# Variance of one LayerNorm tile by a Square with a sum on ScalarE, in a new order of the first phase

## The chip, the cores and the metric

The kernel runs on one core of one Trainium2 chip. The metric is device time in microseconds (us) of one launch, the median over several runs. The core's engines each take their own queue of instructions in order: TensorE (PE, matmuls; its weight loads are shown as PEld), VectorE (DVE), ScalarE (ACT), GpSimd (POOL), and SyncE (SP), which here only issues transfers. They wait for each other through semaphores.

## What is computed

The reference normalises x, a 2048 x 512 matrix in bf16, and adds to x the outputs of two branches that both read the normalised rows:

```python
xn = layernorm(x)                          # over the 512 columns, eps = 1e-5
# branch A: linear attention, 32 heads of 16
q, k, v = split(xn @ wqkv)
pq, pk = phi(q), phi(k)                    # phi(t) = where(t > 0, t + 1, exp(t)) + 1e-6
num = pq @ (pk.T @ v)                      # per head
den = pq . sum(pk) + 1e-6
A = (num / den) @ wo
# branch B: SwiGLU, inner width 1792
B = (silu(xn @ w_gate) * (xn @ w_up)) @ w_down
out = x + A + B
```

## The kernel before

The 2048 rows are cut into 16 tiles of 128 rows, numbered 0 to 15, one row per partition. Phase 1 loads the tiles, normalises each, brings it into transposed form, projects it to k and q, applies phi, and accumulates the product of the normalised tile and phi(k) over all tiles. After that come the gate and up projections of the first 384 rows, the rest of the feed-forward branch in a form that saves products, and the output. The diff touches phase 1 alone, which in the trace lasts until about 48.7 us.

The order of the work in phase 1 is written out by hand: a string of steps, each a letter and a tile number, in the call of `run` at line 536. A step appends its instructions to the queue of the engine that it belongs to. So the place of a step in the string matters only against other steps on the same engine; between engines, the program `_Program.add` (line 53) derives from declared reads and writes which instruction waits for which, and each engine stops at the first instruction whose operands are not there.

The steps that matter below, with tile t:

- S(t), lines 307 and 310, DVE: the statistics of a tile of x (`bn_stats`) and their aggregate `mv`, mean and variance.
- M1, line 334, ACT: a Copy of tile 1 scaled by -1/512 with its sum, which is minus the mean (`negm`).
- R(t), lines 314 and 316, ACT: Ln of the variance plus eps, then Exp of -0.5 times that: `rstd`.
- r(t), lines 321 to 323, ACT: three small operations on one column, `std`, `r2` (one over the variance) and `lstd`. o(t), POOL, makes `flo` and `cap` from `std` (lines 326 and 329).
- Tiles 0 and 1 take a short way: they are only centred (a0, b0: halves of tile 0 on DVE, line 339; C1: tile 1 on DVE with `negm`, line 349), transposed and projected, and the scale `rstd` comes in later, in phi. N0 is a small POOL operation for tile 0.
- The other tiles are normalised in full: L(t) on DVE (line 377), P(t) on POOL (lines 392 and 395), A(t) on ACT.
- c0, d0 (halves of tile 0), W1, W3, X2: transposes on TensorE into a bank of PSUM (line 407). e0 on ACT (line 415), f0, w1, w3, Z2 on DVE (line 417): copies of these banks back to SBUF. From tile 5 on, D(t) on SP transposes by a transfer instead (line 423).
- K(t), k(t): first and second half (two matmuls each for tiles 0 to 3; from tile 4 on k(t) is all four) of the projection to k; Q(t), q(t) the same for q (line 444). Each projection takes the next of banks 4 to 7 in a ring: K0 has 4, K1 5, Q1 6, Q3 7, K3 4 again, then K2 5, Q0 6 and Q2 7.
- x(t), y(t) on ACT: Exp of a projection to k or q (lines 462 and 465). z(t) on ACT: a copy of the q projection (line 454). m(t), n(t) on POOL: a minimum (line 472). s(t) on DVE: phi(k), which reads the bank for the last time and so frees it (line 483); u(t) the same for q.
- J(t) on POOL for tiles 0 and 1: the mean negated into `nmg` (line 369), then xg = (x - mean) times `r2` (line 372), which G(t) needs. G(t), line 493, four matmuls: the product of phi(k) and the normalised tile, accumulated in banks 0 to 3.
- F2: two matmuls on constants that keep TensorE busy (line 297), after eight that stand ahead of the string.

Of the kernel before, what the change touches and what calls it, by code (L numbers as in the profile page):

```python
# [121 lines left out]
def bass_parallel_sum__linear_attn_block__swiglu_ffn__prompt_kernel(nc, A_x, A_wqkv, A_wo, B_x, B_w_gate, B_w_up, B_w_down, out):  # L122
    xin = A_x[0]
    oview = out[0]
    K = _Program()
    bf, f32 = dt.bfloat16, dt.float32

    with contextlib.ExitStack() as es:
        E = es.enter_context

        def sb(name, shape, dtype):
            return E(nc.sbuf_tensor(name, shape, dtype))

# [25 lines left out]
        M = sb("M", [P, NG, D], bf)  # L159
# [112 lines left out]
        for t in range(4, 16):  # L272
# [5 lines left out]
            out=ident[:, :], in_=ident[:, :], compare_op=ALU.not_equal, fill=1.0,  # L278
# [24 lines left out]
        def xk(t):  # L303
            return [("x", 0, 0), ("x", 0, 1)] if t == 0 else [("x", t)]
# [6 lines left out]

        def rs(t):
            sl = slice(t, t + 1)
            K.add("act", lambda e: e.activation(lnv[:, sl], mv[:, t, 1:2], ACT.Ln, bias=eps5[:, :], scale=1.0),
                  r=[("mv", t), ("eps5",)], w=[("lnv", t)])
            K.add("act", lambda e: e.activation(rstd[:, sl], lnv[:, sl], ACT.Exp, scale=-0.5),
                  r=[("lnv", t)], w=[("rs", t)])

# [14 lines left out]
        def neg_mean(t):  # L333
            K.add("act", lambda e: e.activation(
                junk, x_sb[:, t, :], ACT.Copy, scale=-1.0 / D, accum_out=negm[:, t:t + 1]),
                r=xk(t), w=[("negm", t), ("junk",)])

        def centre_half(t, h):
            K.add("dve", lambda e: e.tensor_scalar(
                out=xc[:, t, h * H:(h + 1) * H], in0=x_sb[:, t, h * H:(h + 1) * H], scalar1=mv[:, t, 0:1], scalar2=None,  # L340
                op0=ALU.subtract), r=xk(t) + [("mv", t)], w=[("xc", t, h)])
# [24 lines left out]
                op0=ALU.subtract, op1=ALU.mult), r=xk(t) + [("mv", t), ("r2", t)], w=[("xg", t)])  # L366

        def xg_pool(t):
            K.add("pool", lambda e: e.tensor_scalar(
                out=nmg[:, t:t + 1], in0=mv[:, t, 0:1], scalar1=-1.0, scalar2=0.0, op0=ALU.mult, op1=ALU.add),  # L370
                r=[("mv", t)], w=[("nmg", t)])
            K.add("pool", lambda e: e.tensor_scalar(
                out=xg[:, t, :], in0=x_sb[:, t, :], scalar1=nmg[:, t:t + 1], scalar2=r2[:, t:t + 1],
                op0=ALU.add, op1=ALU.mult), r=xk(t) + [("nmg", t), ("r2", t)], w=[("xg", t)])

        def lna_dve(t):
            K.add("dve", lambda e: e.tensor_scalar(
                out=xn[:, t, :], in0=x_sb[:, t, :], scalar1=mv[:, t, 0:1], scalar2=rstd[:, t:t + 1],
                op0=ALU.subtract, op1=ALU.mult), r=xk(t) + [("mv", t), ("rs", t)], w=[("xn", t)])
# [156 lines left out]
        run("""
            S0 M1 a0 b0 c0 R0 d0 F2 C1 S3 e0 N0 W1 r0 K0 o0 f0 R3 w1 S2 K1 P3 k0 S1 R2 J0 W3 x0 k1 Q1 L2 R1 w3
            m0 X2 q1 r1 Z2 Q3 s0 x1 o1 q3 S5 y1 K3 m1 k3 R5 n1 s1 G0 z1 L5 J1 x3 S9 K2 D5 Q0 z3 m3 S4 k2 R9 q0
            y3 P9 s3 G1 x2 S8 R4 m2 D9 Q2 z0 q2 P4 s2 R8 k5 z2 L8 n3 D4 S15 q5 x5 y0 S12 m5 G2 D8 y5 s5 q9 y2
            n5 S10 R15 k9 n0 y9 u5 R12 n9 k4 x9 L15 u9 D15 q4 m9 x4 L12 R10 s9 m4 q8 y4 D12 S11 P10 k8 z8 s4  # L540
            n4 R11 D10 G9 S13 x8 N11 A11 G5 m8 u4 y8 n2 s8 D11 G3 R13 S14 A0 P13 k15 S7 R14 k12 n8 D13 x15 L14
            S6 m15 q10 x12 D14 s15 m12 k10 y10 s12 n10 k11 x10 u10 R7 m10 q15 x11 s10 q11 m11 y15 L7 R6 s11
            D7 n15 k13 y11 u15 q13 n11 x13 L6 u11 D6 m13 q14 y13 s13 n13 q12 y14 u13 n14 k14 y12 u14 n12 q7
            x14 u12 m14 k7 y7 L1 s14 D0 D1 n7 k6 x7 u0 m7 q6 u7 x6 s7 m6 G4 y6 s6 n6 G12 u2 G14 u6 u1 G6 u8 G10
            u3 G11 G15 G8 G13 G7
        """)
        fload("sp", "wg", wg, B_w_gate, 1)
        wload("sp", 2)
# [304 lines left out]
        X1, X2 = slice(T0, T0 + TB), slice(T0 + TB, S)  # L853
# [507 lines left out]
```

## Time and profile before

| | us |
|---|---|
| median of 3 runs | 199.21 |
| lowest, highest run | 199.07, 199.49 |
| the profiled execution, its own time | 199.49 |
| its span, first to last instruction | 198.2 |
| TensorE busy | 193.8 |
| VectorE busy | 170.6 |
| ScalarE busy | 157.3 |
| GpSimd busy | 127.6 |

The profile is of one execution. The span is shorter than the time by what lies around the program, 1.3 us here. A row of a timeline gives the start and the duration of one instruction, or of a group of like instructions that follow each other, from the start of the first to the end of the last; the last entry is the idle time of the engine before it and what ended that. Instructions on one engine overlap a little at their ends, so a start can lie ahead of the end above it.

### The profile page before, as it was taken

Reading aid. Unit: us, or ns where it says so; the run is one execution under the profiler, and the core shown is the slowest. Engines: PE = TensorE matmul, PEld = TensorE weight load, DVE = VectorE, ACT = ScalarE, POOL = GpSimd, SP = SyncE. Lnnn points to the kernel's source line nnn. Section 1 sums busy time; section 2 is a strip of 40 time slices with the busy share of each in tenths; the row PEclk is TensorE's granted clock in tenths of the full one; section 3 lists DMA queues with packets and bytes.
Section 4 is the critical chain, followed back from the end, with each engine's and each line's share of the span. In section 5 each row is a group of like instructions: output and inputs, shape, how many; then the busy total and the mean of one; then the engine's idle time right before and its main releaser. Section 6 shows DMA issues by size and latency. Waiting matters only on the chain.

```text
span 198.2 us, 3561 instructions
## 1 busy us (share of the span) xinstructions
PE 193.8 (98%) x1193; PEld 115.2 (58%) x1207; DVE 170.6 (86%) x328; ACT 157.3 (79%) x314; POOL 127.6 (64%) x158
## 2 busy tenths in 40 slices
PE   8899999999999999999999999999999999999995
PEld 2344444444655555555555555555555888888884
DVE  2999998896997799887888998887888999998886
ACT  3799888699698998898999888998897967575300
POOL 3687877799999487689778877868579004413220
PEclk9999999999999999999999999999999999999999
DMA  5943248799900000111110221111000012132223
GB/s 171 360 131 81 61 86 231 211 275 373 348 14 0 3 0 0 28 26 30 28 26 2 55 53 26 26 26 31 2 0 2 3 40 66 33 77 66 45 65 121
DMA packets 28899, 15.97 MB, mean 81 GB/s; under 512 B 17232, under 2 KB 28880, under 8 KB 28880
## 3 DMA queue, kind: packets, MB, share of 16 engines
q1 hardware_dynamic: 28320, 15.28, 28.1%
q10 hardware_dynamic: 560, 0.46, 0.7%
q8 instruction: 9, 0.15, 0.3%
q14 instruction: 10, 0.08, 0.1%
HBM read 9.70 MB, written 2.10 MB: 60 GB/s over the span
## 4 chain that ended last, share of the span: by engine, by line
PE 94%; DVE 2%; DMA 2%; issue 1%; ACT 0%; POOL 0%; SPq 0%
PE pb L896 35%; PE pb L1104 16%; PE pb L444 13%; PE pb L565 9%; PE pb L493 7%; PE pb L719 6%; PE pb L1110 5%; DMA x_sb<-in_A_x_dram 2%; PE pb L723 2%; PE pb L625 0%; PE pb L711 0%; DVE pq L483 0%; PE pb L407 0%; POOL ef L472 0%; DVE stats L307 0%
## 5 line engine op out<-in xcount | busy, mean ns | idle before, releaser
L691 POOL TENSOR_TENSOR pq<-pq,rden 128x512 bf16<-128x512 bf16 x16 | 16.9, 1056 | 36.2 <-DVE rden L684 26.7
L896 PE MATMUL pb<-xnT,wgu 128*128 128x416 bf16 x112 | 26.6, 339 | 0.0
L444 PE MATMUL pb<-wqkv,xnT 128*128 128x512 bf16 x110 | 25.1, 379 | 0.2
L665 POOL TENSOR_TENSOR pz<-pq,zbc 128x512 f32<-128x512 bf16 x16 | 18.9, 1180 | 5.1 <-ACT pz L658 3.5
L565 PE MATMUL pb<-xnT,wgu 128*128 128x384 bf16 x112 | 19.9, 326 | 0.1
L931 DVE TENSOR_TENSOR pb<-p,pb 128x416 f32<-128x416 f32 x28 | 16.6, 595 | 3.6 <-PE pb L896 1.9
L472 POOL TENSOR_SCALAR ef<-ef 128x512 bf16<-128x512 bf16 x25 | 15.5, 620 | 5.8 <-ACT ef L465 5.6
L926 ACT ACTIVATE zacc<-pb,iw 128x416 bf16<-128x416 f32 x28 | 16.4, 614 | 3.1 <-PE pb L896 2.3
L444 PEld LDWEIGHTS pb<-wqkv,xnT 128*128 128x128 bf16 x112 | 10.9, 98 | 13.4 <-DVE pk L483 0.4
L936 DVE TENSOR_TENSOR c<-pb,p 128x416 f32<-128x416 f32 x28 | 16.4, 588 | 2.3 <-PE pb L896 0.3
L465 ACT ACTIVATE ef<-pb 128x512 bf16<-128x512 f32 x25 | 14.8, 593 | 3.9 <-PE pb L444 3.9
L940 POOL TENSOR_TENSOR hT<-c,zacc 128x416 bf16<-128x416 f32 x16 | 15.3, 974 | 2.3 <-ACT zacc L926 1.7
L510 POOL TENSOR_TENSOR zacc<-zacc,pk 128x512 f32<-128x512 f32 x13 | 16.0, 1232 | 1.0
L906 ACT ACTIVATE pb<-pb 128x416 f32<-128x416 f32 x28 | 13.7, 501 | 3.0 <-PE pb L896 1.9
L896 PEld LDWEIGHTS pb<-xnT,wgu 128*128 128x128 bf16 x112 | 10.9, 98 | 8.7
L921 ACT ACTIVATE zacc<-pb,iw 128x416 bf16<-128x416 f32 x28 | 15.7, 626 | 0.0
L565 PEld LDWEIGHTS pb<-xnT,wgu 128*128 128x128 bf16 x112 | 10.8, 98 | 7.0 <-DVE xn L613 0.2
L1104 PE MATMUL pb<-wgu,xnT 128*128 128x256 f16 (+1 forms) x112 | 14.9, 273 | 0.0
L896 PE MATMUL pb<-xnT,wqkv 128*128 128x416 bf16 x56 | 14.4, 339 | 0.3
L896 PE MATMUL pb<-wo,wqkv 128*128 128x416 f16 x56 | 14.4, 339 | 0.0
L896 PE MATMUL pb<-GT,wqkv 128*128 128x416 f16 x56 | 14.4, 339 | 0.0
L307 DVE BATCH_NORM_STATS2 stats<-x_sb 128x6 f32<-128x512 bf16 x16 | 10.8, 678 | 3.2 <-DMA x_sb<-in_A_x_dram 3.2
(202 smaller groups left out, 494.1 us busy)
## 6 DMA issues: line engine op xcount, KB each, us to landing
x_sb<-in_A_x_dram SPq DMA_DIRECT2D x14, 128.0 KB, 3.8
wgu<-in_B_w_gate_dram SPq DMA_DIRECT2D x2, 896.0 KB, 5.2
wgu<-in_B_w_up_dram SPq DMA_DIRECT2D x2, 896.0 KB, 8.0
wd<-in_B_w_down_dram SPq DMA_DIRECT2D x2, 896.0 KB, 13.1
out_dram<-out_sb SPq DMA_DIRECT2D x24, 64.0 KB, 1.6
wqkv<-in_A_wqkv_dram SPq DMA_DIRECT2D x3, 256.0 KB, 4.4
wqkv<-in_A_wqkv_dram SPq DMA_DIRECT2D x1, 512.0 KB, 6.3
wo<-in_A_wo_dram SPq DMA_DIRECT2D x1, 512.0 KB, 8.8
```

The lines of the kernel that those rows point to most:

```text
L444: K.add("pe", [(lambda e, c=c: e.matmul(banks[b][:, :], src[:, c, t * P:(t + 1) * P], wqkv[:, c, col:col + D], start=(c == 0), stop=(c == ...
L472: K.add("pool", lambda e: e.tensor_scalar(out=buf, in0=buf, scalar1=top, scalar2=0.0, op0=ALU.min, op1=ALU.max), r=[bkey] + tkeys, w=[bkey])
L510: K.add("pool", lambda e: e.tensor_tensor(out=dst, in0=acc, in1=more, op=ALU.add), r=[key, mkey], w=[dkey])
L565: fns.append(lambda e, c=c, b=b, w_=w_: e.matmul(banks[b][:, 0:T0], w_[:, c, fc * P:(fc + 1) * P], xnT[:, c, 0:T0], start=(c == 0), stop=( ...
L665: K.add("pool", lambda e: e.tensor_tensor(out=halves(i), in0=two(pq[:, t, :]), in1=two(zbc[:, :]), op=ALU.mult), r=[("pq", t), ("zbc",)] + ...
L691: K.add("pool", lambda e: e.tensor_tensor(out=heads(pq[:, t, :]), in0=heads(pq[:, t, :]), in1=rden[:, i, :][:, :, None].broadcast_to([P, N ...
L896: K.add("pe", [(lambda e, c=c: e.matmul(banks[bank][:, 0:TS], L[i][:, c, :], R[i][:, c, ts], start=(start and c == 0), stop=(c == 1), skip ...
L921: K.add("act", lambda e: e.activation(sil4[:, q, :], bk(a), ACT.Silu, scale=iw[:, 0:1]), r=[B(a), ("iw",)], w=[("sil4", q)], a=[("zacc", 0 ...
L926: K.add("act", lambda e: e.activation(sil4[:, 2 + q, :], bk(d), ACT.Silu, scale=iw[:, 0:1]), r=[B(d), ("iw",)], w=[("sil4", 2 + q)], a=[(" ...
L931: K.add("dve", lambda e: e.tensor_tensor(out=bk(d), in0=p5[:, q, :], in1=bk(b), op=ALU.subtract), r=[B(b), ("p5", q)], w=[B(d)])
L936: K.add("dve", lambda e: e.tensor_tensor(out=c22[:, q, :], in0=bk(b), in1=p5[:, q, :], op=ALU.subtract), r=[B(b), ("p5", q)], w=[("c22", q)])
L1104: K.add("pe", [(lambda e, k=k: e.matmul(split(banks[b][:, 0:HD]), L[:, k, :], cut[:, :, k * P:(k + 1) * P], start=(start and k == 0), stop ...
```

## The change

S1, the statistics of tile 1 on VectorE, goes. In its place V1, a Square of (x - mean) over tile 1 on ScalarE, writes its sum into a new column `ssq`; R1 takes the Ln of ssq/512 plus eps. Where tile 1's mean was read from `mv` it is now read as `negm`, with the sign turned: in J1, which so loses its own negation, and in L1, which stands near the end of phase 1. The string of steps is written anew up to about its third line; from `q4` on it is the old one.

```diff
+        ssq = sb("ssq", [P, 2], f32)
...
         def rs(t):
             sl = slice(t, t + 1)
+            if t == 1:
+                K.add("act", lambda e: e.activation(lnv[:, sl], ssq[:, sl], ACT.Ln, bias=eps5[:, :], scale=1.0 / D),
+                      r=[("ssq", t), ("eps5",)], w=[("lnv", t)])
+            else:
+                K.add("act", lambda e: e.activation(lnv[:, sl], mv[:, t, 1:2], ACT.Ln, bias=eps5[:, :], scale=1.0),
+                      r=[("mv", t), ("eps5",)], w=[("lnv", t)])
...
+        def var_act(t):
+            K.add("act", lambda e: e.activation(
+                junk, x_sb[:, t, :], ACT.Square, bias=negm[:, t:t + 1], scale=1.0, accum_out=ssq[:, t:t + 1]),
+                r=xk(t) + [("negm", t)], w=[("ssq", t), ("junk",)])
...
         def xg_pool(t):
+            if t == 1:
+                minus, mkey = negm, ("negm", t)
+            else:
+                minus, mkey = nmg, ("nmg", t)
+                K.add("pool", lambda e: e.tensor_scalar(
+                    out=nmg[:, t:t + 1], in0=mv[:, t, 0:1], scalar1=-1.0, scalar2=0.0, op0=ALU.mult, op1=ALU.add),
+                    r=[("mv", t)], w=[("nmg", t)])
             K.add("pool", lambda e: e.tensor_scalar(
...
-            S0 M1 a0 b0 c0 R0 d0 F2 C1 S3 e0 N0 W1 r0 K0 o0 f0 R3 w1 S2 K1 P3 k0 S1 R2 J0 W3 x0 k1 Q1 L2 R1 w3
-            m0 X2 q1 r1 Z2 Q3 s0 x1 o1 q3 S5 y1 K3 m1 k3 R5 n1 s1 G0 z1 L5 J1 x3 S9 K2 D5 Q0 z3 m3 S4 k2 R9 q0
-            y3 P9 s3 G1 x2 S8 R4 m2 D9 Q2 z0 q2 P4 s2 R8 k5 z2 L8 n3 D4 S15 q5 x5 y0 S12 m5 G2 D8 y5 s5 q9 y2
-            n5 S10 R15 k9 n0 y9 u5 R12 n9 k4 x9 L15 u9 D15 q4 m9 x4 L12 R10 s9 m4 q8 y4 D12 S11 P10 k8 z8 s4
+            S0 a0 b0 M1 R0 r0 F2 c0 C1 e0 d0 N0 o0 W1 S3 R3 K0 w1 f0 P3 k0 V1 J0 K1 S2 k1 W3 R2 L2 x0 R1 w3 X2 Z2 Q1
+            q1 r1 m0 Q3 x1 y1 s0 S5 o1 K3 J1 m1 R5 s1 z1 k3 x3 q3 L5 S9 G0 n1 S8 K2 S4 z3 y3 D5 k2 R9 Q0 m3 P9 D9 x2
+            Q2 s3 R8 R4 m2 s2 L8 q2 P4 q0 z0 S10 D4 G1 z2 k5 x5 n3 q5 y0 m5 G2 y5 y2 S15 S12 n5 s5 n0 q9 R15 k9 y9
+            x9 L15 n9 k4 u5 D8 R12 u9 D15 q4 m9 x4 L12 R10 s9 m4 q8 y4 D12 S11 P10 k8 z8 s4 n4 R11 D10 G9 S13 x8 N11
```

More of the change, by code (lines that the diff above doesn't have):

```diff
@@ L313, in rs @@
             sl = slice(t, t + 1)
-            K.add("act", lambda e: e.activation(lnv[:, sl], mv[:, t, 1:2], ACT.Ln, bias=eps5[:, :], scale=1.0),
-                  r=[("mv", t), ("eps5",)], w=[("lnv", t)])
+            if t == 1:
[4 more added lines that the diff above has]
+                      r=[("mv", t), ("eps5",)], w=[("lnv", t)])
             K.add("act", lambda e: e.activation(rstd[:, sl], lnv[:, sl], ACT.Exp, scale=-0.5),
@@ L368, in xg_pool @@
         def xg_pool(t):
-            K.add("pool", lambda e: e.tensor_scalar(
[L370 to L374, printed above, removed]
-        def lna_dve(t):
+            if t == 1:
[5 more added lines that the diff above has]
+                    r=[("mv", t)], w=[("nmg", t)])
+            K.add("pool", lambda e: e.tensor_scalar(
+                out=xg[:, t, :], in0=x_sb[:, t, :], scalar1=minus[:, t:t + 1], scalar2=r2[:, t:t + 1],
+                op0=ALU.add, op1=ALU.mult), r=xk(t) + [mkey, ("r2", t)], w=[("xg", t)])
+        def lna_dve(t):
+            if t == 1:
+                K.add("dve", lambda e: e.tensor_scalar(
+                    out=xn[:, t, :], in0=x_sb[:, t, :], scalar1=negm[:, t:t + 1], scalar2=rstd[:, t:t + 1],
+                    op0=ALU.add, op1=ALU.mult), r=xk(t) + [("negm", t), ("rs", t)], w=[("xn", t)])
+                return
             K.add("dve", lambda e: e.tensor_scalar(
@@ L518, in bass_parallel_sum__linear_attn_block__swiglu_ffn__prompt_kernel @@
             "S": stat, "R": rs, "L": lna_dve, "P": lna_pool, "N": nmr, "A": lna_act, "D": dmat,
-            "M": neg_mean, "a": lambda t: centre_half(t, 0), "b": lambda t: centre_half(t, 1),
+            "M": neg_mean, "V": var_act, "a": lambda t: centre_half(t, 0), "b": lambda t: centre_half(t, 1),
             "I": centre_mv, "C": centre_dve, "B": centre_act, "E": centre_pool, "r": powers, "o": floor, "j": xg_dve, "J": xg_pool,
@@ L536, in bass_parallel_sum__linear_attn_block__swiglu_ffn__prompt_kernel @@
         run("""
-            S0 M1 a0 b0 c0 R0 d0 F2 C1 S3 e0 N0 W1 r0 K0 o0 f0 R3 w1 S2 K1 P3 k0 S1 R2 J0 W3 x0 k1 Q1 L2 R1 w3
-            m0 X2 q1 r1 Z2 Q3 s0 x1 o1 q3 S5 y1 K3 m1 k3 R5 n1 s1 G0 z1 L5 J1 x3 S9 K2 D5 Q0 z3 m3 S4 k2 R9 q0
-            y3 P9 s3 G1 x2 S8 R4 m2 D9 Q2 z0 q2 P4 s2 R8 k5 z2 L8 n3 D4 S15 q5 x5 y0 S12 m5 G2 D8 y5 s5 q9 y2
-            n5 S10 R15 k9 n0 y9 u5 R12 n9 k4 x9 L15 u9 D15 q4 m9 x4 L12 R10 s9 m4 q8 y4 D12 S11 P10 k8 z8 s4
[L541 to L545, printed above, removed]
+            S0 a0 b0 M1 R0 r0 F2 c0 C1 e0 d0 N0 o0 W1 S3 R3 K0 w1 f0 P3 k0 V1 J0 K1 S2 k1 W3 R2 L2 x0 R1 w3 X2 Z2 Q1
+            q1 r1 m0 Q3 x1 y1 s0 S5 o1 K3 J1 m1 R5 s1 z1 k3 x3 q3 L5 S9 G0 n1 S8 K2 S4 z3 y3 D5 k2 R9 Q0 m3 P9 D9 x2
+            Q2 s3 R8 R4 m2 s2 L8 q2 P4 q0 z0 S10 D4 G1 z2 k5 x5 n3 q5 y0 m5 G2 y5 y2 S15 S12 n5 s5 n0 q9 R15 k9 y9
+            x9 L15 n9 k4 u5 D8 R12 u9 D15 q4 m9 x4 L12 R10 s9 m4 q8 y4 D12 S11 P10 k8 z8 s4 n4 R11 D10 G9 S13 x8 N11
+            A11 G5 m8 u4 y8 n2 s8 D11 G3 R13 S14 A0 P13 k15 S7 R14 k12 n8 D13 x15 L14 S6 m15 q10 x12 D14 s15 m12 k10
+            y10 s12 n10 k11 x10 u10 R7 m10 q15 x11 s10 q11 m11 y15 L7 R6 s11 D7 n15 k13 y11 u15 q13 n11 x13 L6 u11
+            D6 m13 q14 y13 s13 n13 q12 y14 u13 n14 k14 y12 u14 n12 q7 x14 u12 m14 k7 y7 L1 s14 D0 D1 n7 k6 x7 u0 m7
+            q6 u7 x6 s7 m6 G4 y6 s6 n6 G12 u2 G14 u6 u1 G6 u8 G10 u3 G11 G15 G8 G13 G7
         """)
```

## The prediction

> **What bounds the kernel now.** I read the page first (busy time by engine, the chain that ended last), then the waits of TensorE, then the timeline of the first 20 us, because the diff touches only phase 1.
>
> ```profile
> PE 193.8 (98%) x1193; PEld 115.2 (58%) x1207; DVE 170.6 (86%) x328; ACT 157.3 (79%) x314; POOL 127.6 (64%) x158
> ...
> PE 94%; DVE 2%; DMA 2%; issue 1%; ACT 0%; POOL 0%; SPq 0%
> ```
>
> ```profile
> PE pb L297 <- PEq L1346: 0.8, 1, 0.8
> PE pb L444 <- DVE hT L417: 0.3, 1, 0.3
> PE pb L407 <- DVE hT L349: 0.3, 1, 0.3
> ```
>
> TensorE is 98% busy and is 94% of the chain; the three lines (total, times, longest) are the whole list of its waits. After 0.8 us at the start it idles twice for 0.3 us. So the time is the useful matmul work plus the holes before it becomes dense, and only a change in those holes can move the end. The list is blind to small holes, since a matmul's row is longer than the step from one matmul to the next; those show only in the starts. The timeline of TensorE (start, duration, engine, line, operation, tiles, count, idle before):
>
> ```profile
> 5.50 0.40 PE L407 MATMUL pb<-ident,hT 128*128 128x128 bf16 x4 [0.31 <-DVE hT L349]
> 5.89 0.59 PE L444 MATMUL pb<-wqkv,hT 128*128 128x512 bf16 x2
> 6.82 1.04 PE L444 MATMUL pb<-wqkv,hT 128*128 128x512 bf16 x4 [0.34 <-DVE hT L417]
> 7.83 0.40 PE L407 MATMUL pb<-ident,xn 128*128 128x128 bf16 x4
> 8.06 1.03 PE L444 MATMUL pb<-wqkv,hT 128*128 128x512 bf16 x4
> 9.00 0.40 PE L407 MATMUL pb<-ident,xn 128*128 128x128 bf16 x4
> 9.23 0.59 PE L444 MATMUL pb<-wqkv,hT 128*128 128x512 bf16 x2
> 9.66 1.95 PE L444 MATMUL pb<-wqkv,xnT 128*128 128x512 bf16 x8
> 11.45 0.81 PE L493 MATMUL pb<-pk,hT 128*128 128x512 bf16 x3
> 12.31 0.59 PE L444 MATMUL pb<-wqkv,xnT 128*128 128x512 bf16 x2
> ...
> 14.90 2.75 PE L444 MATMUL pb<-wqkv,xnT 128*128 128x512 bf16 x12
> 17.49 1.03 PE L493 MATMUL pb<-pk,xn 128*128 128x512 bf16 x4
> ```
>
> and, from a narrower window, the second half of the eight at 9.66:
>
> ```profile
> 10.58 1.04 PE L444 MATMUL pb<-wqkv,xnT 128*128 128x512 bf16 x4
> ```
>
> From 14.90 to 17.49 twelve matmuls take 2.59 us, 0.216 each: that is the dense pace. A group of four transposes takes 0.23 (9.00 to 9.23). Counting on from 6.82 in the order of the string: K1 and k0, four matmuls, are through by 7.70 (the first step after a wait is a little longer) and W3 starts at 7.83, a hole of 0.13; k1 and Q1 are through by 8.92 and X2 starts at 9.00 (0.08); q1, Q3, q3 by 10.53 and K3 starts at 10.58 (0.05). Then K3, k3 and the four of G0 (one record is missing) lead to K2 at 12.31, and from there to 14.90 another twelve take 2.59. No hole is left. All holes after 6.82 together are 0.26 us: that is all that the new order could win there.
>
> **The change part by part.** The other engines in the same stretch, ScalarE first:
>
> ```profile
> 4.33 0.63 ACT L334 ACTIVATE hT<-x_sb 128x512 bf16<-128x512 bf16 x1 [2.25 <-DMA x_sb<-in_A_x_dram]
> ...
> 5.38 0.36 ACT L415 ACTIVATE hT<-pb 128x256 bf16<-128x256 bf16 x1
> ...
> 6.62 0.20 ACT L316 ACTIVATE rstd<-lnv 128x1 f32<-128x1 f32 x1
> 7.62 0.29 ACT L314 ACTIVATE lnv<-mv,eps 128x1 f32<-128x1 f32 x1 [0.80 <-DVE mv L310]
> 7.94 0.20 ACT L316 ACTIVATE rstd<-lnv 128x1 f32<-128x1 f32 x1
> 8.05 0.76 ACT L462 ACTIVATE ef<-pb,lstd,rstd 128x512 bf16<-128x512 f32 x1
> ...
> 12.76 0.60 ACT L454 ACTIVATE hT<-pb 128x512 f32<-128x512 f32 x1
> ```
>
> VectorE:
>
> ```profile
> 6.18 0.59 DVE L417 COPY hT<-pb 128x256 bf16<-128x256 bf16 x2
> ...
> 7.50 0.66 DVE L307 BATCH_NORM_STATS2 stats<-x_sb 128x6 f32<-128x512 bf16 x1
> ...
> 8.29 0.65 DVE L377 TENSOR_SCALAR xn<-x_sb,mv,rstd 128x512 bf16<-128x512 bf16 x1
> ...
> 9.78 0.74 DVE L483 SCALAR_TENSOR_TENSOR pk<-pb,flo,ef 128x512 bf16<-128x512 f32 x1
> ...
> 11.93 0.41 DVE L377 TENSOR_SCALAR xn<-x_sb,mv,rstd 128x512 bf16<-128x512 bf16 x1
> ...
> 16.10 0.51 DVE L377 TENSOR_SCALAR xn<-x_sb,mv,rstd 128x512 bf16<-128x512 bf16 x1
> ...
> 20.16 0.70 DVE L377 TENSOR_SCALAR xn<-x_sb,mv,rstd 128x512 bf16<-128x512 bf16 x1
> ```
>
> POOL:
>
> ```profile
> 8.04 0.76 POOL L372 TENSOR_SCALAR hT<-x_sb,nmg,r 128x512 bf16<-128x512 bf16 x1
> 8.91 0.68 POOL L472 TENSOR_SCALAR ef<-ef,cap 128x512 bf16<-128x512 bf16 x1
> ...
> 9.96 0.19 POOL L329 TENSOR_SCALAR cap<-std 128x1 f32<-128x1 f32 x1
> ...
> 12.11 0.88 POOL L372 TENSOR_SCALAR hT<-x_sb,nmg,r 128x512 bf16<-128x512 bf16 x1
> ...
> 15.70 0.77 POOL L395 TENSOR_SCALAR xn<-x_sb,nm,rstd 128x512 bf16<-128x512 bf16 x1
> ...
> 20.10 0.61 POOL L472 TENSOR_SCALAR ef<-ef 128x512 bf16<-128x512 bf16 x1 [0.16 <-ACT ef L465]
> ```
>
> *Removed: S1.* The statistics of tile 1 (row 7.50) and their aggregate held DVE until L2 began at 8.29, 0.79 us. L2, the LayerNorm of tile 2, also needs rstd of tile 2, which ScalarE delivers at 8.14 (row 7.94). So L2 may now start near 8.18 instead of 8.29: 0.11 won at its start, and no more.
>
> *Added: V1.* A Square with a sum over 512 elements. The trace has no Square in this stretch; the nearest row is M1, a Copy with a sum over the same tile (4.33, 0.63 us). V1 also takes its bias from a column, and an Exp on 512 elements with two such operands takes 0.76 (row 8.05). The floor is therefore 0.63, and as a ceiling I add the Exp whole: 1.39. I take 0.72, near M1, since one column operand is all that sets them apart. V1 starts behind rstd of tile 3 (row 6.62, ending 6.82) and ends near 7.5. ScalarE idles until 7.62 there, 0.80 us waiting for mv of tile 2, and that idle time hides V1. At the ceiling rstd of tile 2 would come 0.5 us late. R1 keeps its place behind x0, and its Ln reads ssq instead of mv, at the same cost.
>
> *Moved at the front: F2 before c0, r0 before e0, w1 before f0.* Four small ScalarE operations stand in another order with e0 last, which puts K0 at about 6.07 instead of 5.89 (e0: row 5.38, now some 0.2 later). That costs nothing: K0's two matmuls are through by 6.50, and k0, next in the new order, waits for f0, the second of two copies that end at 6.77 (row 6.18) whichever comes first. The dense stretch begins at 6.82 as before, with the same work ahead of it; without that cover K0 would cost 0.18. F2 and the transposes c0 and d0 have time until 5.50, where W1 waits for the centring of tile 1 in any case.
>
> *Moved: X2 ahead of Q1.* This is the part that decides. TensorE now runs k0 K1 k1 (six matmuls), W3, X2, Q1, q1, Q3, K3, k3, q3, G0. Six from 6.82 are through by 8.13; W3, whose operand was there for 7.83, by 8.36. X2 transposes what L2 writes. When does L2 end? It took 0.65 from 8.29, beside xg of tile 0 on POOL, which ran to 8.80. At 16.10 the same operation took 0.51 beside a POOL operation that ended at 16.47; at 20.16 it took 0.70 beside one that ended at 20.71; at 11.93 it took 0.41. The three disturbed ones ended at 8.94, 16.61 and 20.86: each time 0.14 or 0.15 after POOL's end, whatever their length. So L2 does not run slower, it is held until POOL lets go, and a start at 8.18, still behind xg's 8.04, changes nothing: it ends at 8.94. P3 and J0, ahead of it on POOL, keep their order and their inputs. X2 stays at 9.00.
>
> The Trainium skill, page "SBUF — State Buffer", section "SBUF: two separate sides", says that VectorE and GpSimd share one pair of ports under an exclusive lock: the operation that starts first keeps it for its whole length and the other blocks fully. By that X2 starts at 9.00; read instead as a stretch to 0.65 us wherever L2 starts, the same row would give 8.89. The three ends agree with the page.
>
> So TensorE idles from 8.36 to 9.00, 0.64 us, while Q1, whose operands are there, stands behind X2 in the queue. Q1 q1 Q3, six matmuls from 9.23, are through by 10.53. K3 needs bank 4, which s0 frees (row 9.78); s0 stands on DVE behind Z2, which waits for X2, so both stay, and K3 starts at 10.58 as before. But q3, which used to run before K3, now comes after k3: 2 x 0.216 = 0.43 us. G0 moves from 11.45 to 11.88, K2 from 12.31 to 12.74. Counted by holes it is the same: 0.64 + 0.05 instead of 0.26.
>
> *Moved on POOL: J1 ahead of m1, without its negated mean.* xg of tile 1 (0.88 in row 12.11, 0.76 for tile 0 in row 8.04) now follows cap (9.96) and runs from 10.24 to 11.00 or 11.12. m1 (0.68 like m0, row 8.91) ends at 11.7 or 11.8, s1 (0.74 like s0) at 12.41 to 12.55. K2 needs bank 5 from s1 and comes at 12.74: no wait, but a thin cover; an s1 later than 12.69 would hold K2.
>
> *Moved behind it.* L5 stands behind s1 on DVE, so the transpose of tile 5, the first on SP, goes out late:
>
> ```profile
> 12.37 9.70 SPq L423 DMA_TRANSPOSE xnT<-xn  x5
> ```
>
> ```profile
> xnT<-xn SPq DMA_TRANSPOSE x14, 2.5
> ```
>
> Issued near 12.8 instead of 12.37, it lands 2.5 us later, at 15.3; its user k5 comes 16 matmuls behind K2, at 12.74 + 16 x 0.216 = 16.19, and does not wait. SP's own order is unchanged. y3 moves ahead of R9 on ScalarE, straight behind z3 (row 12.76, ending 13.36), and ends near 13.85, in time for Q2 at 12.74 + 6 x 0.216 = 14.03. From q4 on the string is the old one, and all of it follows TensorE.
>
> *Sum.* +0.43 us on the profiled execution: its time of 199.49 becomes 199.92, its span of 198.2 becomes 198.6. It is the slowest of the three runs, 0.28 above their median of 199.21; on the median I forecast 199.64.
>
> **The rivals.**
> - *The forecast: Q1 queued behind X2, 199.64.* For it: TensorE takes its queue in order, and X2's start hangs on L2's end alone. Chance 0.52.
> - *L2 is not held.* With its own 0.41, or stretched to 0.65, it ends at 8.59 to 8.83. The next gate is s0: m0 ends at 9.59 (row 8.91) whatever X2 does, s0 takes 0.74 and two hand-overs, K3 starts at 10.42 at the earliest, and the shift is 0.43 - 0.16 = 0.27: 199.48. Against it: the three equal distances. 0.14.
> - *POOL's new order becomes a wait.* If xg and DVE's LayerNorm or copies hold each other up once more by 0.4 us, s1 ends near 12.95 and K2 waits 0.3 beyond the forecast: 199.94. It decides from 0.15 us of extra delay on. 0.13.
> - *V1 is not hidden.* At the ceiling rstd of tile 2 and x0 come 0.5 late; x0 drags m0 and s0, whose slack against m0 is 0.19 (9.59 to 9.78), and K3 with them: 0.31 more, 199.95. Against it: 0.80 us of idle time. 0.07.
> - *Faster: a freed DVE closes the holes.* If L2, or the copies at 6.18, come earlier than these rows let me see, the holes of 0.26 go, and the 0.34 ahead of 6.82 with them: 198.61. It decides if L2 ends by 8.30. For it: DVE is 0.79 us lighter in the stretch where TensorE waits for it. Against it: S1 stood behind both copies, and rstd comes at 8.14. 0.14.
>
> **How the numbers follow.** The likeliest case gives 199.64. A measurement of this kernel can tell about 0.2%, 0.4 us, from no change, so "within" is 198.81 to 199.61. The three runs scatter by some 0.2, so of the forecast's 0.52 I put 0.35 above that bound and 0.17 below. Slower: 0.35 + 0.13 + 0.07 = 0.55. Within: 0.17 + 0.14 + 0.02 = 0.33, the 0.02 from a faster case cut short. Faster: 0.12. The range 198.9 to 200.1 leaves out most of the faster case and the far tails of the last two slower ones. The forecast's own range is 199.45 to 199.85.
>
> **What would show it.** Right: K0 near 6.07, six matmuls from 6.82, X2 at 9.00 with an idle of about 0.4 named before it, K3 near 10.58, K2 near 12.74 and an unbroken pace behind; V1 between 6.7 and 7.6 with Ln of tile 2 still at 7.62; L2 ending 0.14 after POOL's xg. Wrong: X2 before 8.9 (L2 was free), K2 waiting for s1 (POOL's order), Ln of tile 2 after 7.7 (V1 in the way), or a new wait of TensorE behind 12.74, of which I have counted none.

## The result, and the profile after

The changed kernel takes 199.65 us (median of 22 runs, 199.34 to 200.1), the kernel before, run beside it, 199.19 (22 runs, 198.88 to 200.02). The ratio is 1.0019, with a 95% interval of 1.0011 to 1.0028: slower by 0.46 us by the medians, by 0.2 to 0.6 us by the interval. The forecast was 199.64.

The profiled execution of the changed kernel took 199.45 us with a span of 198.2, the same span as that of before. The reason stands in its timeline of ScalarE: tile 1 of x landed early in this execution, and M1, which needs it, started at 3.91 instead of 4.33. Everything at the front therefore lies 0.42 us earlier than in the profile of before, and the forecast's times are compared less 0.42. Two lines of the page, busy time by engine and the chain that ended last by engine:

```profile
PE 194.1 (98%) x1207; PEld 115.7 (58%) x1207; DVE 170.2 (86%) x326; ACT 158.3 (80%) x316; POOL 127.3 (64%) x157
...
PE 95%; DVE 2%; DMA 1%; issue 0%; ACT 0%; SPq 0%
```

VectorE lost 0.4 us, ScalarE gained 1.0: the sum of squares did change engines. TensorE's busy time is within 0.3 us of what it was, so the loss is to be looked for in its holes. The waits of TensorE (total, times, longest), the whole list:

```profile
PE pb L298 <- PEq L1364: 0.8, 1, 0.8
PE pb L426 <- DVE xn L396: 0.5, 1, 0.5
PE pb L426 <- DVE hT L359: 0.4, 1, 0.4
PE pb L463 <- ACT hT L434: 0.2, 1, 0.2
```

The second line is new. L426 is the transpose, `xn` from L396 is what L2 writes: X2 waits for L2. The fourth is K0 behind e0, which the forecast put 0.18 later. The timeline of TensorE shows where (start, duration, operation, count, idle time before it):

```profile
5.65 2.22 PE L463 MATMUL pb<-wqkv,hT 128*128 128x512 bf16 x8 [0.18 <-ACT hT L434]
7.71 0.39 PE L426 MATMUL pb<-ident,xn 128*128 128x128 bf16 x4
8.58 0.40 PE L426 MATMUL pb<-ident,xn 128*128 128x128 bf16 x4 [0.49 <-DVE xn L396]
8.81 1.03 PE L463 MATMUL pb<-wqkv,hT 128*128 128x512 bf16 x4
9.68 1.95 PE L463 MATMUL pb<-wqkv,xnT 128*128 128x512 bf16 x8
11.46 1.03 PE L512 MATMUL pb<-pk,hT 128*128 128x512 bf16 x4
12.32 1.03 PE L463 MATMUL pb<-wqkv,xnT 128*128 128x512 bf16 x4
```

Two narrower windows give the start of the dense stretch behind K0 and, inside the group at 9.68, the start of K3:

```profile
6.40 1.47 PE L463 MATMUL pb<-wqkv,hT 128*128 128x512 bf16 x6
```

```profile
10.15 1.04 PE L463 MATMUL pb<-wqkv,xnT 128*128 128x512 bf16 x4
```

From 6.40 six matmuls lead to W3 at 7.71 without a hole. W3, a group of four transposes, is through 0.23 later, at 7.94, and X2 starts at 8.58: a hole of 0.64. Q1 q1 Q3 from 8.81 are through by 8.81 + 6 x 0.216 = 10.11, and K3 starts at 10.15. From the dense start to K2 it is now 12.32 - 6.40 = 5.92 us; before it was 12.31 - 6.82 = 5.49. That is the 0.43 of the forecast, and the early landing of x hides it in this one span.

The rows on the other engines that set this; ScalarE:

```profile
3.91 0.63 ACT L339 ACTIVATE hT<-x_sb 128x512 bf16<-128x512 bf16 x1 [1.83 <-DMA x_sb<-in_A_x_dram]
...
6.31 0.71 ACT L344 ACTIVATE hT<-x_sb,negm 128x512 bf16<-128x512 bf16 x1
6.92 0.19 ACT L344 ACTIVATION_READ_ACCUMULATOR hT<-x_sb,negm 128x1 f32 x1
7.20 0.29 ACT L319 ACTIVATE lnv<-mv,eps 128x1 f32<-128x1 f32 x1
```

VectorE and POOL:

```profile
6.98 0.18 DVE L311 BATCH_NORM_AGGREGATE mv<-stats 128x2 f32<-128x6 f32 x1
7.76 0.76 DVE L396 TENSOR_SCALAR xn<-x_sb,mv,rstd 128x512 bf16<-128x512 bf16 x1 [0.60 <-ACT rstd L321]
...
11.18 0.75 DVE L502 SCALAR_TENSOR_TENSOR pk<-pb,flo,ef 128x512 bf16<-128x512 f32 x1 [0.26 <-POOL ef L491]
```

```profile
7.62 0.76 POOL L386 TENSOR_SCALAR hT<-x_sb,nmg,r 128x512 bf16<-128x512 bf16 x1
```

V1 (6.31) takes 0.71 with a read of its sum until 7.11 behind it, and the Ln of tile 2 starts at 7.20, 0.04 behind its `mv` (6.98 + 0.18): V1 delays nothing. VectorE idles 0.60 us ahead of L2, where S1 was. And L2 starts at 7.76, 0.11 earlier than in the old frame (8.29 - 0.42 = 7.87), lasts 0.76 and ends at 8.52, 0.14 behind xg of tile 0 on POOL (7.62 + 0.76 = 8.38). What S1's absence gave was taken back by a longer L2.

### The profile page after: what moved, and what is told of

It is laid out like the page before. It is cut to its first block, busy times and chain, and to the rows that moved or that the text cites. A ratio compares the mean times of both kernels' runs of the same rounds, so it can differ in the third digit from the quotient of the medians.

```text
span 198.2 us, 3575 instructions
## 1 busy us (share of the span) xinstructions
PE 194.1 (98%) x1207; PEld 115.7 (58%) x1207; DVE 170.2 (86%) x326; ACT 158.3 (80%) x316; POOL 127.3 (64%) x157
## 4 chain that ended last, share of the span: by engine, by line
PE 95%; DVE 2%; DMA 1%; issue 0%; ACT 0%; SPq 0%
PE pb L914 35%; PE pb L1122 16%; PE pb L463 13%; PE pb L583 9%; PE pb L512 7%; PE pb L737 6%; PE pb L1128 5%; PE pb L741 2%; DMA x_sb<-in_A_x_dram 1%; DVE stats L308 1%; PE pb L643 0%; PE pb L729 0%; DVE xn L396 0%; DVE hT L436 0%; DVE out_sb L1154 0%
## 5 line engine op out<-in xcount | busy, mean ns | idle before, releaser
L1128 PE MATMUL pb<-M,pk 128*128 128x256 bf16 x96 | 13.6, 273 | 0.0
```

The costliest lines, as they stand in the source:

```text
L1128: K.add("pe", [(lambda e, g=g: e.matmul(dk(b), pk[:, SLOT[t], g * P:(g + 1) * P], M[:, g, lo:lo + HD], start=False, stop=(g == NG - 1), sk ...
```

## The experiments

All times are medians, beside runs of the kernel before on the same chip. Where a diff shows steps only, these are the stretches of the string that differ, in order. The ratio and its interval are those on record, from all the runs of both kernels; the ratio is not the quotient of the two medians. The holes are those of TensorE behind its dense start, counted from the starts in the timeline as above.

| run | us | before | ratio, 95% interval |
|---|---|---|---|
| changed kernel | 199.65 | 199.19 | 1.0019, 1.0011 to 1.0028 |
| X2 behind Q1 | 199.84 | 199.23 | 1.0032, 1.0007 to 1.0057 |
| q3 ahead of K3 | 199.68 | 199.23 | 1.0015, 0.9992 to 1.0037 |
| both | 199.44 | 199.23 | 1.0002, 0.9982 to 1.0022 |
| TensorE's whole old order | 199.28 | 199.23 | 1.0008, 0.9998 to 1.0018 |
| before, X2 ahead of Q1 | 199.55 | 199.23 | 1.0017, 1.0008 to 1.0026 |
| before, Square for S1 | 199.16 | 199.23 | 0.9986, 0.9960 to 1.0011 |
| before, Square, xg of tile 0 on VectorE | 199.34 | 199.23 | 1.0001, 0.9993 to 1.0010 |
| changed kernel, Square twice | 199.93 | 199.09 | 1.0038, 1.0025 to 1.0051 |
| the same again | 199.98 | 199.08 | 1.0049, 1.0026 to 1.0073 |
| early front | 199.95 | 199.23 | 1.0047, 1.0028 to 1.0066 |
| copy on ScalarE | 199.37 | 199.09 | 1.0017, 1.0002 to 1.0033 |
| the same again | 199.18 | 199.08 | 1.0014, 0.9994 to 1.0034 |

**One half of the new order undone: X2 behind Q1.** From the changed kernel:

```diff
-w3 X2 Z2 Q1 q1
+w3 Q1 X2 Z2 q1
```

> The changed kernel with X2 and Z2 behind Q1 as before, q3 still behind k3. Theory (two steps of the queue share the loss): Q1 fills part of the hole ahead of X2, which shrinks from 0.64 to about 0.21, but K3 then comes too early for s0 and waits 0.48; K2 stands where it stands in the changed kernel, so no gain: +0.43 us on before, ratio 1.0022. Rival (X2's place alone is the loss): the 0.43 is won back, ratio 1.000. Rival (V1 or POOL's order is the loss): ratio as the changed kernel, with the idle time somewhere else than before X2 and K3.

The timeline of TensorE in this run:

```profile
8.04 0.39 PE L426 MATMUL pb<-ident,xn 128*128 128x128 bf16 x4
8.27 0.59 PE L463 MATMUL pb<-wqkv,hT 128*128 128x512 bf16 x2
8.91 0.40 PE L426 MATMUL pb<-ident,xn 128*128 128x128 bf16 x4
...
9.58 0.59 PE L463 MATMUL pb<-wqkv,xnT 128*128 128x512 bf16 x2
10.49 1.47 PE L463 MATMUL pb<-wqkv,xnT 128*128 128x512 bf16 x6 [0.32 <-DVE pk L502]
```

Q1 now runs ahead of X2, and X2's hole shrinks from 0.64 to 0.21 (8.27 + 0.43 = 8.70 to 8.91). But K3 needs the bank that s0 frees and cannot come earlier, so the two matmuls taken out of the first hole leave a second one of 0.48 ahead of K3 (9.58 + 0.43 = 10.01 to 10.49). The sum is again 0.69, and the time does not improve.

**The other half: q3 ahead of K3.**

```diff
-o1 K3 J1 m1 R5 s1 z1 k3 x3 q3 L5
+o1 q3 K3 J1 m1 R5 s1 z1 k3 x3 L5
```

> The changed kernel with q3 ahead of K3 as before, X2 still ahead of Q1. Theory: the hole of 0.64 ahead of X2 stays, eight matmuls follow it and K3 does not wait at all, so 0.05 is won of 0.43: about +0.38 us on before, ratio 1.0019. Rival (q3's place alone): 1.000.

X2's hole stays at 0.65 (W3 from 8.38 through 8.61, X2 at 9.26 in this run's timeline), K3 has no hole, so 0.04 of the 0.69 is gone. The median is that of the changed kernel; the ratio's interval, 0.9992 to 1.0037, is too wide to decide, and it is the holes that show it: neither move alone gives back more than 0.04.

**Both.** The two edits above together.

> The changed kernel with both steps where they were, so with TensorE's old holes and all else changed (Square on ScalarE, no statistics of tile 1 on VectorE, J1 ahead of m1, r0 ahead of e0). Theory: a hole of 0.21 ahead of X2 and of 0.05 ahead of K3, 0.26 in all as before: ratio 1.000 within 0.0005. Rival (V1 not hidden, or POOL's new order): ratio stays at 1.002.

The median is still 0.21 above that of before, and the interval, 0.9982 to 1.0022, holds 1.000 as well as the changed kernel's 1.0019: the times of this run do not decide. Nor was the picture the expected one. In this execution the second half of K's weights landed late, so that the dense stretch began late, at 6.74, and X2 found its operand ready. And a hole that I had not counted stands at Q2; TensorE first, then ScalarE:

```profile
12.86 0.59 PE L463 MATMUL pb<-wqkv,hT 128*128 128x512 bf16 x2
13.58 1.04 PE L463 MATMUL pb<-wqkv,xnT 128*128 128x512 bf16 x4
```

```profile
12.44 0.60 ACT L473 ACTIVATE hT<-pb 128x512 f32<-128x512 f32 x1
12.91 0.61 ACT L484 ACTIVATE pq<-pb 128x512 bf16<-128x512 f32 x1
```

The two matmuls at 12.86 are through at 13.29; Q2 comes at 13.58, behind y3, which ends at 13.52: 0.29. The new string puts Q2 earlier in TensorE's queue than the old one, and in the changed kernel that costs nothing only because everything there comes 0.43 late.

**TensorE's queue as before, the rest of the new string kept.** The diff shows the moved stretches:

```diff
-r0 F2 c0 C1 e0 d0 N0
+r0 c0 d0 C1 e0 F2 N0
...
-P3 k0 V1 J0 K1 S2 k1 W3 R2
+P3 K1 V1 J0 k0 S2 W3 k1 R2
...
-w3 X2 Z2 Q1 q1
+w3 Q1 X2 Z2 q1
...
-o1 K3 J1 m1 R5 s1 z1 k3 x3 q3 L5
+o1 q3 J1 m1 R5 s1 z1 K3 k3 x3 L5
...
-D5 k2 R9 Q0 m3 P9 D9 x2 Q2 s3 R8 R4 m2 s2 L8 q2 P4 q0 z0 S10 D4 G1 z2
+D5 Q0 R9 k2 m3 P9 D9 x2 q0 s3 R8 R4 m2 s2 L8 G1 P4 Q2 z0 S10 D4 q2 z2
```

> The changed kernel with TensorE's whole queue in the order of the kernel before (F2, k0 and K1, X2, q3, and also K2 Q0 k2 q0 G1 Q2); all other engines keep the changed order, but for Z2 and x3, which have to stay behind X2 and k3. The run with X2 and q3 alone put back showed a third hole of 0.29 us ahead of Q2, which in the changed order comes before q0 and G1 and so needs y3 early. Theory: with TensorE's order old, that hole goes as well, and K2 alone may wait up to 0.1 for s1, since J1 is still ahead of m1: +0.0 to +0.1 us, ratio 1.0000 to 1.0005. Rival (the order of the other engines costs something by itself): ratio stays near 1.002.

```profile
11.95 0.60 PE L463 MATMUL pb<-wqkv,xnT 128*128 128x512 bf16 x2
```

The hole at Q2 is gone. K2 starts at 11.95, behind four matmuls of G0 from 11.00 that are through at 11.86, so it waits 0.09 for s1, which ends at 11.14 + 0.75 = 11.89. From the start of M1 (3.87) to K2 it is 8.08 us; in the profile of before it is 12.31 - 4.33 = 7.98, in that of the changed kernel 12.32 - 3.91 = 8.41. So TensorE's old order wins 0.33 of the 0.43 back, with V1 and the new orders of the other engines in place, and the 0.1 left is K2's wait, since J1 still stands ahead of m1. The times agree, but they are no sharp proof: the ratio is 1.0008 and its interval holds 1.0, though its upper end lies above the lower end of the changed kernel's.

**The converse: only X2 ahead of Q1, in the kernel before.**

```diff
-x0 k1 Q1 L2 R1 w3 m0 X2 q1
+x0 k1 L2 R1 w3 m0 X2 Q1 q1
```

> The kernel before, statistics of tile 1 on VectorE as they were, with Q1 moved behind X2 on TensorE and nothing else. Theory: the order alone makes the loss: W3 and k1 end at 8.49 in the frame of the profile of before, a hole of 0.51 to X2 at 9.00, then eight matmuls and K3 without a wait: +0.38 us, ratio 1.0019. Rival (it is the Square or POOL's order): 1.000.

```profile
7.47 0.40 PE L407 MATMUL pb<-ident,xn 128*128 128x128 bf16 x4
7.70 0.59 PE L444 MATMUL pb<-wqkv,hT 128*128 128x512 bf16 x2
8.64 0.40 PE L407 MATMUL pb<-ident,xn 128*128 128x128 bf16 x4 [0.35 <-DVE xn L377]
8.88 1.03 PE L444 MATMUL pb<-wqkv,hT 128*128 128x512 bf16 x4
9.74 1.89 PE L444 MATMUL pb<-wqkv,xnT 128*128 128x512 bf16 x8
```

X2 waits from 8.13 (7.70 + 0.43) to 8.64, 0.51. With the 0.14 ahead of W3 the holes are 0.65 instead of 0.26, and the time is +0.3 by medians, 0.2 to 0.5 by the interval. This one move, without V1, makes a loss of 0.39 by the holes, where the whole change has 0.43.

**Only the Square, in the old order.** The string of before with `S1` replaced by `V1`, and the changed functions:

```diff
-P3 k0 S1 R2 J0 W3
+P3 k0 V1 R2 J0 W3
```

> The kernel before with V1 in the place of S1 and nothing else moved. Theory: V1 hides in ScalarE's wait, L2 may start 0.11 earlier but is held by POOL's xg and ends at the same time; ratio 1.000, L2 ending 0.14 after xg. Rival (VectorE's relief shortens the way): X2 0.11 earlier and at most 0.08 won, ratio 0.9996. Rival (V1 delays rstd of tile 2): ratio above 1.001 with Ln of tile 2 late.

Taking the statistics off VectorE gains nothing that can be measured. L2 lasts 0.76 there too and ends at 8.92, 0.14 behind xg's end at 8.78.

**L2 without its neighbour on POOL.** The same kernel, with xg of tile 0 computed by VectorE (`j0`) behind w3 instead of by POOL (`J0`):

```diff
-P3 k0 S1 R2 J0 W3
+P3 k0 V1 R2 W3
...
-R1 w3 m0
+R1 w3 j0 m0
```

> The kernel before with V1 for S1, and xg of tile 0 made by VectorE behind w3 instead of POOL beside L2. If L2 is held by POOL's xg: L2 now lasts 0.40 to 0.42 instead of 0.65 to 0.76, ends near 8.6 in the frame of before, and the holes ahead of X2 and K3 shrink from 0.13 to about 0.03: -0.1 us, ratio 0.9995. If L2 is slow for another reason, it keeps 0.65 or more and X2 stays.

VectorE, then TensorE:

```profile
7.93 0.41 DVE L396 TENSOR_SCALAR xn<-x_sb,mv,rstd 128x512 bf16<-128x512 bf16 x1 [0.60 <-ACT rstd L321]
```

```profile
7.81 1.03 PE L463 MATMUL pb<-wqkv,hT 128*128 128x512 bf16 x4
8.68 0.39 PE L426 MATMUL pb<-ident,xn 128*128 128x128 bf16 x4
...
9.33 2.01 PE L463 MATMUL pb<-wqkv,xnT 128*128 128x512 bf16 x8
11.18 0.59 PE L512 MATMUL pb<-pk,hT 128*128 128x512 bf16 x2
```

With the same operands at the same place L2 takes 0.41 instead of 0.76, and X2 starts at 8.68, at the dense pace behind 7.81 + 4 x 0.216: no hole. So L2 was held by POOL's xg. That an operation of one of these two engines holds up one of the other is what the Trainium skill, page "SBUF — State Buffer", section "SBUF: two separate sides", has; how far the hold reaches is in the last section. The 0.1 us expected from it did not come: the eight matmuls from 9.33 should be through at 11.06, G0 starts at 11.18, so a hole of 0.12 has opened ahead of K3 among them, which still waits for s0 (it ends at 9.50 + 0.75 = 10.25). The hole moved from X2 to K3. In part the hold itself turned round; POOL:

```profile
8.66 0.81 POOL L491 TENSOR_SCALAR ef<-ef,cap 128x512 bf16<-128x512 bf16 x1 [1.14 <-ACT ef L481]
```

This is m0, which s0 needs. It starts 0.07 behind `j0` on VectorE (8.59, 0.40) and lasts 0.81, where it took 0.68 in the kernel before.

**A second Square.** To measure how much cover V1 has left, the changed kernel runs it twice; the additional one writes to places that nobody reads.

```diff
         def var_act(t):
             K.add("act", lambda e: e.activation(
+                hT[:, 1, 7, :], x_sb[:, t, :], ACT.Square, bias=negm[:, t:t + 1], scale=1.0, accum_out=ssq[:, 0:1]),
+                r=xk(t) + [("negm", t)], w=[("ssq", 0), ("junk",)])
+            K.add("act", lambda e: e.activation(
                 junk, x_sb[:, t, :], ACT.Square, bias=negm[:, t:t + 1], scale=1.0, accum_out=ssq[:, t:t + 1]),
```

> The changed kernel with a second Square of the same kind directly ahead of V1 (it writes to places that nothing reads). In the profile of the changed kernel V1 and its read of the sum end at 7.11 and Ln of tile 2 starts at 7.20, released by mv at 7.16: the cover of V1 is down to 0.1 us. Theory: the second one is not covered; Ln of tile 2 comes 0.6 late, L2 is then held by nothing and ends 0.27 later, x0, m0, s0 and K3 come 0.47 later: +0.47 us on the changed kernel, 1.0045 on before. Rival (ScalarE has room): no change on the changed kernel, 1.002 on before.

The median is 0.84 above that of the kernel before beside it; with one Square it was 0.46. The profile of this run was taken in an execution with late weights (last section), so I ran the kernel again:

> The kernel of the run with two Squares once more, because its profile fell into an execution of 201.18 us, 1.25 above its median, in which K0 waited for the weights and the next matmuls came 0.43 us apart instead of 0.216. Theory (the cover of V1 was used up, so a second Square of 0.71 is on the path): with the weights in time, Ln of tile 2 starts 0.5 to 0.6 us behind the end of its mv, L2 takes its own 0.41 because xg on POOL has its ports before it, the hole ahead of X2 is 0.8 to 0.9 us instead of 0.64, K3's a further 0.3, and the median is again 199.9 (ratio 1.004). Rival (the slow stretch of that profile belongs to this kernel): matmuls 0.43 us apart are found again behind K0, and the median is above 200.5.

ScalarE and VectorE of the second run:

```profile
6.48 0.71 ACT L344 ACTIVATE hT<-x_sb,negm 128x512 bf16<-128x512 bf16 x1
...
7.18 0.71 ACT L347 ACTIVATE hT<-x_sb,negm 128x512 bf16<-128x512 bf16 x1
...
7.88 0.28 ACT L319 ACTIVATE lnv<-mv,eps 128x1 f32<-128x1 f32 x1
```

```profile
7.15 0.18 DVE L311 BATCH_NORM_AGGREGATE mv<-stats 128x2 f32<-128x6 f32 x1
8.43 0.41 DVE L399 TENSOR_SCALAR xn<-x_sb,mv,rstd 128x512 bf16<-128x512 bf16 x1 [1.10 <-ACT rstd L321]
```

`mv` of tile 2 is there at 7.33, its Ln starts at 7.88, 0.55 behind it instead of 0.04, and the median is 0.90 above that of the kernel before: one Square fits under the wait, a second does not. The expected hole of 0.8 ahead of X2 was a miss: the dense stretch itself began late here, at 7.12, with W3 at 8.42 and X2 at 8.90, a hole of 0.25. The delay can be seen from the landing of tile 1 instead: K2 (12.86) comes 8.78 behind the start of M1 (4.08); in the changed kernel it is 12.32 - 3.91 = 8.41. That makes 0.37, of the size of the 0.31 that the prediction gave for a V1 that is not hidden. The late dense start is not what made it: K3 starts at 10.69, 0.26 after Q3 is through (10.00 + 0.43), so it waits for s0 (9.88 + 0.75 = 10.63). And s0 hangs on x0 and m0 on the other engines: it starts 5.80 behind M1, where it is 9.36 - 3.91 = 5.45 in the changed kernel.

**Two attempts to beat both kernels.** The first puts the copy f0 on ScalarE (`h0`), k0, k1, Q1 and q1 ahead of W3, and V1 behind R2:

```diff
-e0 N0 W1 r0 K0 o0 f0 R3 w1 S2 K1 P3 k0 S1 R2 J0 W3 x0 k1 Q1 L2 R1 w3 m0 X2 q1 r1 Z2 Q3 s0 x1
+e0 h0 N0 W1 r0 K0 o0 J0 k0 R3 w1 S2 P3 K1 k1 x0 Q1 R2 V1 q1 W3 L2 R1 w3 m0 X2 r1 Q3 s0 Z2 x1
```

> An attempt to beat both kernels: V1 for S1, behind R2; f0 replaced by a copy on ScalarE (straight behind e0), so that k0 need not wait for VectorE; TensorE runs K0 k0 K1 k1 Q1 q1 W3 X2 Q3 q3; x0 ahead of R2, xg of tile 0 ahead of P3 on POOL, s0 ahead of Z2. By rows of the trace of before: K0 at 5.9, eight matmuls of tile 0 and 1 and Q1, q1 without a hole to 8.47, X2 at 8.70, a hole of 0.4 to Q3 that waits for w3, K3 near 10.2 instead of 10.58, K2 near 12.0 instead of 12.31, waiting for s1: -0.3 us, ratio 0.9985. If the landing of the weights holds k0 or q1, less of it.

A miss, slower than both. ScalarE and VectorE:

```profile
9.34 0.29 ACT L316 ACTIVATE lnv<-ssq,eps 128x1 f32<-128x1 f32 x1
...
10.19 0.78 ACT L481 ACTIVATE ef<-pb,lstd,rstd 128x512 bf16<-128x512 f32 x1
```

```profile
11.85 0.75 DVE L502 SCALAR_TENSOR_TENSOR pk<-pb,flo,ef 128x512 bf16<-128x512 f32 x1 [0.26 <-POOL ef L491]
```

Behind R2, V1 has no wait to hide in. It pushes Ln of tile 1 to 9.34 and x1 to 10.19, where the changed kernel has 9.12 with tile 1 landed 0.21 earlier; s1 ends at 12.60, and K2, which needs its bank, starts at 12.66.

The second is gentler: the string of before with V1 for S1, xg of tile 0 on VectorE, and only the copy f0 moved to ScalarE.

```diff
-e0 N0 W1 r0 K0 o0 f0 R3 w1 S2 K1 P3 k0 S1 R2 J0 W3 x0 k1 Q1 L2 R1 w3 m0
+e0 h0 N0 W1 r0 K0 o0 k0 R3 w1 S2 K1 P3 k1 V1 R2 W3 x0 Q1 L2 R1 w3 j0 m0
```

> The version with V1 for S1 and xg of tile 0 on VectorE, and in addition f0 replaced by a copy on ScalarE straight behind e0, k0 straight behind K0 and k1 ahead of W3 on TensorE. Unlike the earlier attempt, x0, V1 and R2 keep their places. In the frame of the profile of before: K0 5.89, k0 as soon as its weights land (6.3 to 6.6), K1 and k1 behind it by 7.7, W3 7.83, Q1, X2 near 8.57, q1 Q3 q3, K3 near 10.33 instead of 10.58, held by s0: -0.25 us, ratio 0.9987. If only the landing of the weights and of x sets the front, 1.000.

Slower instead, with K0 at 6.71, 1.04 us idle ahead of it. I ran it again to see whether that wait is its own:

> The kernel of the run with the copy on ScalarE once more. Theory (its late K0 at 6.71 was a late landing of the first weights in that one execution): with the weights landing by 6.3, K0 starts at 6.0 to 6.2 and TensorE is dense from there, the span of the profile is at most 198.0, and the median is 199.0 to 199.2. Rival (the wait belongs to this kernel's own order on ScalarE): K0 starts 0.1 behind rstd of tile 3 again, at 6.6 or later with the x of tile 1 landing as before, and the median is again 199.3 to 199.5.

The timeline of TensorE in the second run:

```profile
6.21 1.90 PE L463 MATMUL pb<-wqkv,hT 128*128 128x512 bf16 x8
...
10.70 1.04 PE L463 MATMUL pb<-wqkv,xnT 128*128 128x512 bf16 x4 [0.19 <-DVE pk L502]
...
12.43 0.59 PE L463 MATMUL pb<-wqkv,xnT 128*128 128x512 bf16 x2
```

K0 starts at 6.21 although tile 1 landed late (M1 at 4.66), and K1 and k0 follow without a hole: the rival fell. From M1 to K2 it is 7.77, against 7.98 before, so 0.21 is won in the trace. The times do not show it: a median of 199.18 lay in the expected band, but the ratio's interval, 0.9994 to 1.0034, has no room for 0.2 us of gain, and the span of 198.3 was above the 198.0 expected, with tile 1 0.33 later than in the profile of before. Where the 0.21 goes over many executions is not settled; no version beat the kernel before.

## Why the prediction was right

*TensorE's order.* "TensorE idles from 8.36 to 9.00, 0.64 us, while Q1 stands behind X2 in the queue": measured 0.64, from 7.94 to 8.58 in a frame 0.42 earlier. K0 at 5.65 and the dense start at 6.40 are 6.07 and 6.82 less 0.42; X2, K3 and K2 came 0.42 or 0.43 before their forecast times. The move alone, in the kernel before, gives 0.39 of it, and TensorE's old order in the changed kernel takes all but 0.1 away. So this mechanism is shown, not only argued. The size, 0.43, was 0.46 by the medians and lies inside the interval. That the forecast of 199.64 met the median of 199.65 to 0.01 is luck: it was built on a median of three runs, and the runs of each kernel scatter over some 0.8 us or more.

*What was not seen as such:* X2's place is not the only one that costs. X2 ahead of Q1 makes the loss by itself, but to put X2 back alone wins nothing, because q3 behind k3 makes it as well. The experiments show a pair of gates, L2's end ahead of X2 and s0's end ahead of K3, with a fixed amount of work to fill the gaps. Q1 and q3 must both stand ahead of their gate; either one behind it makes 0.39 to 0.43.

*Removed: S1.* "0.11 won at its start, and no more", then lost in L2's hold: measured exactly so. The hold itself is shown by L2's 0.41 once POOL is out of the way. The rival in which L2 is not held named s0 as the next gate; with L2 free, the hole did move to K3. That the three ends "agree with the page" (the Trainium skill, page "SBUF — State Buffer", section "SBUF: two separate sides": the other operation fully blocks) holds for the hold, not for its length: an L2 blocked until 8.80 that then took its own 0.41 would have ended at 9.21, not at 8.94.

*Added: V1.* Taken at 0.72, measured 0.71 and hidden. But its cover was thinner than the row of 0.80 idle suggests: the read of the sum behind V1, which the forecast did not count, ends 0.80 us after V1's start (7.11 - 6.31), and 0.09 us were left between it and the Ln of tile 2. The rival with V1 not hidden is what the second Square made: 0.37 in the trace and about 0.4 in the medians, for its price of 0.31.

*Moved on POOL.* xg of tile 1 ahead of m1 made no wait: s1 ended at 11.93 (11.18 + 0.75), or 12.35 in the forecast's frame, a little ahead of the 12.41 to 12.55 given, and G0 and K2 did not wait. The rival with POOL's order fell. The thin cover shows where TensorE's order is the old one and K2 comes earlier: there K2 waited 0.09 for s1.

*The step that held for a thin reason* is y3 "in time for Q2". It is true in the changed kernel, with 0.18 us to spare in the forecast, and only since Q2 is itself 0.43 late; the run with both moves undone paid 0.29 there. A forecast of that version from the same page should have asked it.

## What to carry to other kernels

An engine with an in-order queue waits at the first instruction that is not ready, so in a hand-written order each gated instruction wants exactly the work ahead of it that fills the time to its gate; before moving one, list the gates behind it and count the work between them. Taking work off an engine that is not the bound gains nothing until one has found which operation ends its successor's wait: here it was an operation on another engine, whose end, not its own length, set L2's. And read a change of 0.2% from many runs and from distances inside the trace, not from the spans of two profiles: these were equal here.

## What the hardware showed that was not expected

*How a held operation looks.* L2 ended 0.14 or 0.15 us behind POOL's operation in each profile in which it started well before that one's end, and its row simply gets longer, with no idle time before it. But in the run with two Squares it started 0.11 us before xg's end (8.43, POOL's xg being 7.78 + 0.76 = 8.54) and kept its 0.41. So in these rows the hold reaches only the last 0.14 us of the row, and the 0.27 us ahead of that run beside POOL. Whether those 0.27 us are a start-up or part of the work, the rows do not tell. The rule of the Trainium skill, page "SBUF — State Buffer", section "SBUF: two separate sides", that the other operation fully blocks fits them only if nothing but those 0.14 us needs the ports.

*The landing of the first loads moves the front.* M1, which waits for tile 1, started between 3.73 and 4.66 in the profiles of these kernels, which issue the same loads in the same order. TensorE is named as waiting for weights in four, by 0.2 to 0.7 us. That is as much as the change is worth, and it is why single spans could not be compared.

*TensorE at half pace.* The first profile of the kernel with two Squares fell into an execution of 201.18 us. Its wait of TensorE for weights, and two of the weight loads behind it:

```profile
PE pb L466 <- DMA wqkv<-in_A_wqkv_dram: 0.7, 1, 0.7
```

```profile
7.84 0.15 PEld L466 LDWEIGHTS pb<-wqkv,hT 128*128 128x128 bf16 x1 [0.27 <-issue]
8.27 0.15 PEld L466 LDWEIGHTS pb<-wqkv,hT 128*128 128x128 bf16 x1 [0.28 <-issue]
```

The loads, and with them the matmuls, come 0.42 us apart instead of 0.216, until 9.97, although the granted clock is given as 1.00 throughout. From 7.43 to 9.97 that is six steps of 0.42, or 6 x (0.42 - 0.216) = 1.2 us more than at the dense pace. The execution lies 1.25 above the median of 199.93, but that is not the same sum: at the dense pace W3 would have been through at 8.96 and X2 would have waited for L2, which ended at 8.69 + 0.41 = 9.10, so at most 1.1 of the 1.2 can count. The Trainium skill, page "TensorE: Matmul & The Clock Gate", section "Part 1: The HAM clock gate", gives 426.7 ns between matmuls of this size for the cold array and 215.7 for the warm one, which agrees. The page lets the clock fall after an idle window of about 3.4 us. No pause of that length stands ahead of these steps, and no 128x512 matmul ahead of 9.97 is at the fast pace: the constants from 0.84 on come 0.43 apart, and the rows of the projections last 0.59 to 0.63 us, where they last 0.38 or 0.39 in the profile of the changed kernel. So by these rows the pace had not fallen but had not yet risen, although the ten matmuls on constants had run. In the profiles of before and after the projections are fast from the first one on, at 5.89 and 5.65. Why the pace rose so late in this execution is not shown.
